# Attention and gated MLP on one core: the start of the x tiles moved by 32 bytes

## The chip, the cores and the metric

One core of a Trainium2 chip runs the whole program. The metric is device time in microseconds (us); a run's time is that of this one core.

## What is computed

```
B, H, S, D = 8, 8, 576, 64          # batch, heads, tokens, head width
scores = q @ k.T / sqrt(D)          # masked: heads 0-3 see 32 tokens back, heads 4-7 every 32nd token back
attn   = softmax(scores);  y = attn @ v
x = y.transpose(0, 2, 1, 3).reshape(B * S, H * D)       # 4608 x 512
h = x @ w_in                                            # 512 -> 2048
sp = max(h, 0) + log1p(exp(-abs(h)));  g = h * erf(sp)
out = g @ w_out                                         # 2048 -> 512, float32
```

## The kernel before

**Staging.** Attention runs a batch entry and a pair of heads at a time (`heads`, L324): scores into PSUM (L400), maximum, difference, exponential, sum and division on the vector, scalar and GpSimd engines, a transpose on TensorE (L507), and the product with v (L526). The result, 128 channels by 576 tokens, is split into two float32r parts that together carry float32 precision: ScalarE casts the upper part into `xhi` (L545), VectorE writes what is left into `xlo` (L550). There are four tiles of each, one per pair of heads, each with room for two batch entries of 576 tokens (`RING`, 1152 words in a partition).

**The MLP** works on chunks of 512 tokens: one chunk for each of the eight batch entries, and a ninth of the 64 tokens that each entry leaves over, which go out to memory (`stash`, L842) and come back (`reload`, L848). A chunk is done in 16 tiles of 128 of the 2048 hidden features (`ftile`, L665). One such f-tile has two groups of 12 matmuls, all 128 x 128 by 128 x 512, on float32r operands:

- `mm1` (L679): the stationary operand is a 128 x 128 block of a `pair` tile of `w_in` (upper or lower part), the moving operand 512 columns of `xhi` or `xlo`, in the order: upper weights with the four `xhi`, lower weights with the four `xhi`, upper weights with the four `xlo`. All 12 add up in one PSUM bank.
- `mm2` (L755): for each of four blocks of 128 tokens, three matmuls. The stationary operand is a 128 x 128 block of `ghi`, `ghi` again, and `glo`; the moving operand is the upper, the lower and again the upper half of a `pair` tile of `w_out`.

Between them ScalarE and VectorE turn h into g in ten passes over 128 x 512 (L687, L693, L684, L717, L720, L723). Over the run `mm1` and `mm2` have 1728 matmuls each, 144 groups of 12.

**Order.** A planner (`Plan`, L158) lays all operations of all engines out in time from tables of keys (`KP`, `KW`, `FT`), costs and buffer counts, and the program is issued in that order. The planner does not know addresses.

**Addresses.** Tiles of a pool lie one after another in each partition, and a tile's size is rounded up to 32 bytes. Pool `cpool` comes first: `xhi` and `xlo` (4608 bytes each), `ident` (512), `con` (1024; masks and a bf16 identity), `con_e` (one word, 32 bytes taken; the zero that the first exponential is taken of, to load ScalarE's table, L803 and L806). In the built program the x tiles start at byte 16512 of a partition, a multiple of 64, and since 4608 is one too, so do all eight, `ident`, `con` and `con_e`. The 32 bytes of `con_e` then put every tile of the later pools, the `pair`, `ghi`, `glo`, `qk`, `sm` tiles and all others, 32 bytes past a multiple of 64. The second batch entry of an x tile starts 2304 bytes on, again a multiple of 64; a block of 128 columns of a stationary operand is 512 bytes wide.

Of the kernel before, what the change touches and what calls it, by code (L numbers as in the profile page):

```python
# [8 lines left out]
F32 = mybir.dt.float32  # L9
# [9 lines left out]
P = 128  # L19
# [247 lines left out]
def attention_moe(  # L267
# [15 lines left out]
    cpool = ctx.enter_context(tc.tile_pool(name="cpool", bufs=1))  # L283
# [4 lines left out]
    ps_h = ctx.enter_context(tc.tile_pool(name="ps_h", bufs=2, space=PSUM))  # L288
    ps_o = ctx.enter_context(tc.tile_pool(name="ps_o", bufs=1, space=PSUM))

    xhi = [cpool.tile([P, RING], F32R, name=f"xhi{c}") for c in range(NCC)]
    xlo = [cpool.tile([P, RING], F32R, name=f"xlo{c}") for c in range(NCC)]
    ident = cpool.tile([P, P], F32, name="ident")
    con = cpool.tile([P, NCON], BF16, name="con")
    con_e = cpool.tile([P, 1], F32, name="con_e")
    mask_l = con[:, :320]
    mask_s = con[:, 320:384].rearrange("p (u q) -> p u q", u=1)
    ident_b = con[:, 384:]
# [688 lines left out]
```

## Time and profile before

| what | value |
|---|---|
| median of 3 runs (lowest to highest) | 940.04 us (939.42 to 943.2) |
| the profiled execution, its own time | 937.79 us |
| its span, first to last instruction | 936.0 us |
| TensorE matmuls busy | 909.9 us (97%) |
| TensorE weight loads busy | 728.6 us (78%) |
| VectorE busy | 680.5 us (73%) |
| ScalarE busy | 687.7 us (73%) |
| GpSimd busy | 69.7 us (7%) |
| DMA, mean rate | 77 GB/s |
| mean granted TensorE clock, share of full speed | 0.995 |

The engines are PE (TensorE's matmuls), PEld (its weight loads, which run beside the matmuls), ACT (ScalarE), DVE (VectorE), POOL (GpSimd) and SP (SyncE, which issues most DMAs). Matmuls are pipelined: the duration of one in the profile covers its way through the array and overlaps with that of the next, so the time that a matmul costs is the distance from its start to the start of the next. In a timeline row that merges several matmuls, the start is that of the first and the duration reaches to the end of the last.

### The profile page before, as it was taken

To read this page: it belongs to the slowest core of one execution; us is meant where nothing else is said; L and a number is where in the kernel's file an instruction comes from. 1 tells how busy PE (TensorE), PEld (TensorE's weight loads), DVE (VectorE), ACT (ScalarE), POOL (GpSimd) and SP (SyncE) were. 2 spreads that over 40 slices of the span, in tenths; PEclk is the share of its full clock that TensorE was granted. 3 is DMA by queue.
4 is the path that set the end of the run, shared out by engine and by line. 5 is a ranking of instruction groups with operands and counts; after the bars stand their busy time and mean duration, and the time that the engine had idled before them with its cause. 6 is when DMAs were issued, how large, how long until landed. Compare 5 with 4: busy or idle time off the path is not lost.

```text
span 936.0 us, 18645 instructions
## 1 busy us (share of the span) xinstructions
PE 909.9 (97%) x7589; PEld 728.6 (78%) x7593; DVE 680.5 (73%) x1111; ACT 687.7 (73%) x1330; POOL 69.7 (7%) x66
## 2 busy tenths in 40 slices
PE   5789999999999999999999999999999999999997
PEld 3567888788878788887878888878888888888885
DVE  7999998988578757766588666685687656665653
ACT  4798988887686767776777668767777687768773
POOL 1310012002021000000010010010001100000000
PEclk9899999999999999999999999999999999999999
DMA  9995123314142202011222021021221310001002
GB/s 346 314 352 210 45 66 52 67 56 99 32 86 72 69 29 103 28 47 48 77 85 68 27 89 46 28 91 34 71 85 41 93 46 1 1 1 45 1 1 45
DMA packets 33557, 72.43 MB, mean 77 GB/s; under 512 B 11968, under 2 KB 12608, under 8 KB 33472
## 3 DMA queue, kind: packets, MB, share of 16 engines
q1 hardware_dynamic: 30016, 64.96, 20.4%
q0 software_dynamic: 3456, 6.29, 3.9%
q8 instruction: 59, 0.97, 0.4%
q14 instruction: 26, 0.21, 0.1%
HBM read 55.51 MB, written 15.73 MB: 76 GB/s over the span
## 4 chain that ended last, share of the span: by engine, by line
PE 83%; issue 5%; DVE 5%; DMA 4%; ACT 2%; SPq 0%; POOL 0%; ACTq 0%; POOLq 0%; DVEq 0%
PE o L755 38%; PE h L679 38%; PE x L526 3%; PE s L400 2%; DMA qk<-qk_str 2%; PE t L507 1%; DVE a L684 1%; ACT a L687 1%; DMA words<-w_in 1%; DMA out<-ob 1%; DVE glo L723 1%; DMA v<-v_str 0%; DVE hs L717 0%; DVE mx L436 0%; PE s L526 0%
## 5 line engine op out<-in xcount | busy, mean ns | idle before, releaser
L755 PE MATMUL o<-pair,ghi 128*128 128x512 f32 x1152 | 364.1, 397 | 0.4 <-ACT ob L771 0.4
L687 ACT ACTIVATE a<-a 128x512 f32<-128x512 f32 x432 | 262.8, 631 | 52.5 <-DVE a L684 51.2
L679 PE MATMUL h<-xhi,pair 128*128 128x512 f32 x1152 | 294.2, 397 | 0.2 <-DVE a L684 0.2
L679 PEld LDWEIGHTS h<-xhi,pair 128*128 128x128 f32 x1152 | 214.7, 188 | 52.2 <-DVE a L684 1.3
L755 PEld LDWEIGHTS o<-pair,ghi 128*128 128x128 f32 x1152 | 211.6, 188 | 46.9 <-ACT ob L771 0.9
L755 PE MATMUL o<-pair,glo 128*128 128x512 f32 x576 | 224.9, 390 | 0.4 <-DVE glo L723 0.2
L679 PE MATMUL h<-xlo,pair 128*128 128x512 f32 x576 | 157.6, 395 | 0.0
L723 DVE TENSOR_TENSOR glo<-hs,ghi 128x512 fp32r<-128x512 f32 x144 | 102.6, 713 | 71.6 <-ACT ghi L720 71.3
L717 DVE TENSOR_TENSOR hs<-a,hs 128x512 f32<-128x512 f32 x144 | 105.7, 734 | 63.5 <-ACT a L687 63.5
L687 ACT ACTIVATE a<-h 128x512 f32<-128x512 f32 x144 | 86.2, 598 | 75.4 <-PE h L679 62.8
L684 DVE SCALAR_TENSOR_TENSOR a<-a,hs 128x512 f32<-128x512 f32 x144 | 99.4, 690 | 47.0 <-ACT hs L693 33.1
L679 PEld LDWEIGHTS h<-xlo,pair 128*128 128x128 f32 x576 | 108.2, 188 | 26.2
L755 PEld LDWEIGHTS o<-pair,glo 128*128 128x128 f32 x576 | 108.2, 188 | 25.2 <-DVE glo L723 1.2
L684 DVE SCALAR_TENSOR_TENSOR a<-h,a 128x512 f32<-128x512 f32 x144 | 98.8, 686 | 31.9 <-ACT a L687 16.9
L693 ACT COPY hs<-h 128x512 f32<-128x512 f32 x144 | 84.3, 585 | 46.4 <-DVE glo L723 43.9
L720 ACT CAST ghi<-hs 128x512 fp32r<-128x512 f32 x144 | 88.4, 614 | 22.2 <-PE o L755 20.8
L684 DVE SCALAR_TENSOR_TENSOR a<-b,a 128x512 f32<-128x512 f32 x144 | 100.5, 698 | 2.1
L687 ACT ACTIVATE b<-a 128x512 f32<-128x512 f32 x144 | 89.9, 624 | 0.4
L498 POOL TENSOR_TENSOR sm<-sm,r 128x768 f32<-128x768 f32 (+3 forms) x37 | 51.0, 1379 | 513.7 <-DVE r L491 478.2
L771 ACT COPY ob<-o 128x512 f32<-128x512 f32 x52 | 30.1, 589 | 9.7 <-DMA out<-ob 4.3
L526 PEld LDWEIGHTS x<-sm,v 64*64 64x64 f32 x1392 | 24.4, 134 | 9.2 <-ACT sm L513 7.0
L436 DVE TENSOR_REDUCE mx<-s 128x12 f32<-128x768 f32 (+3 forms) x37 | 28.9, 782 | 0.3
(50 smaller groups left out, 506.1 us busy)
## 6 DMA issues: line engine op xcount, KB each, us to landing
v<-v_loc SPq DMA_DIRECT2D x13, 640.0 KB, 4.0
words<-w_in SPq DMA_DIRECT2D x16, 512.0 KB, 6.5
words<-w_out SPq DMA_DIRECT2D x16, 512.0 KB, 8.2
out<-ob SPq DMA_DIRECT2D x32, 256.0 KB, 2.0
qk<-qk_loc SPq DMA_DIRECT2D x13, 592.0 KB, 4.1
qk<-qk_str SPq DMA_DIRECT2D x12, 608.0 KB, 3.8
v<-v_str SPq DMA_DIRECT2D x16, 384.0 KB, 3.5
out<-ob POOLq DMA_DIRECT2D x16, 256.0 KB, 5.0
```

Source lines behind the costliest of these rows:

```text
L436: yield nc.vector.tensor_reduce(out=mx[:, parts[i], :units], in_=wide(of(s, i)), axis=mybir.AxisListType.X, op=ALU.max)
L498: yield (nc.gpsimd if pool_norm else nc.vector).tensor_tensor(out=d, in0=d, in1=spread(rc, i), op=ALU.mult)
L526: yield nc.tensor.matmul(bank(px, m)[h * D : (h + 1) * D, a * n : (a + 1) * n], values(rows, (2 * a + h) * D), pt[rows, h, c : c + n], sta ...
L679: yield nc.tensor.matmul(ph[:, :CH], win[4 * s + cc][:, w, fs], x[cc][:, c0 : c0 + CH], start=(i == 0), stop=(i == len(terms) - 1))
L684: yield nc.vector.scalar_tensor_tensor(out=out, in0=in0, scalar=scalar, in1=in1, op0=op0, op1=op1)
L687: yield nc.scalar.activation(dst, src, func, bias=bias[i], scale=scale)
L693: yield nc.scalar.copy(hs.tile, ph.tile)
L717: yield nc.vector.tensor_tensor(out=hs.tile, in0=a.tile, in1=hs.tile, op=ALU.mult)
L720: yield nc.scalar.copy(ghi.tile, hs.tile)
L723: yield nc.vector.tensor_tensor(out=glo.tile, in0=hs.tile, in1=ghi.tile.bitcast(F32), op=ALU.subtract)
L755: yield nc.tensor.matmul(po.tile, g[:, ts], wout[f][:, w], start=(f == first_f and i == 0), stop=(f == last_f and i == 2),)
L771: yield nc.scalar.copy(ob.tile, po.tile)
```

## The change

A tile `shift` of 8 words (32 bytes) is allocated ahead of the x tiles, and `con_e`, which stood behind `con`, becomes its first word.

```diff
+    shift = cpool.tile([P, 8], F32, name="shift")
     xhi = [cpool.tile([P, RING], F32R, name=f"xhi{c}") for c in range(NCC)]
     xlo = [cpool.tile([P, RING], F32R, name=f"xlo{c}") for c in range(NCC)]
     ident = cpool.tile([P, P], F32, name="ident")
     con = cpool.tile([P, NCON], BF16, name="con")
-    con_e = cpool.tile([P, 1], F32, name="con_e")
+    con_e = shift[:, :1]
```

In the program built from it, `shift` starts at byte 16512 and the eight x tiles, `ident` and `con` each start 32 bytes later than before, 32 bytes past a multiple of 64. The later pools start at the same byte as before (54944), and none of their tiles moves. On every engine the same instructions stand in the same order with the same waits; the memset and the first exponential name `shift` where they named `con_e`, and that is all that differs.

## Rows read from the trace of the kernel before

**Rows 1.** The page's list of engines: busy us, share of the span, instructions.
```profile
PE 909.9 (97%) x7589; PEld 728.6 (78%) x7593; DVE 680.5 (73%) x1111; ACT 687.7 (73%) x1330; POOL 69.7 (7%) x66
```

**Rows 2.** Busy time of each engine by stretch; PEclk is the granted clock.
```profile
core 0: us, PE busy (x) PEld busy (x) DVE busy (x) ACT busy (x) POOL busy (x), PEclk, DMA share, GB/s
...
50.00:100.00 50.00, 47.11 (x457) 37.17 (x457) 49.18 (x89) 44.26 (x99) 3.43 (x3) 1.00 0.68 248
100.00:200.00 100.00, 99.56 (x650) 80.32 (x649) 93.67 (x161) 84.89 (x155) 9.64 (x10) 1.00 0.24 52
...
800.00:900.00 100.00, 100.00 (x434) 81.30 (x433) 59.80 (x90) 73.52 (x131) 0.00 (x0) 1.00 0.03 11
```

**Rows 3.** Waits of PE from 100 us on: total us, times, longest us.
```profile
PE x L526 <- ACT sm L513: 0.4, 1, 0.4
PE o L755 <- ACT ob L771: 0.4, 1, 0.4
PE o L755 <- DVE glo L723: 0.2, 1, 0.2
```

**Rows 4.** Groups by form: busy us, mean ns of one | idle us before, releaser.
```profile
L755 PE MATMUL o<-pair,ghi 128*128 128x512 f32 x1152 | 364.1, 397 | 0.4 <-ACT ob L771 0.4
L679 PE MATMUL h<-xhi,pair 128*128 128x512 f32 x1152 | 294.2, 397 | 0.2 <-DVE a L684 0.2
```

**Rows 5.** Timeline of PE, one f-tile of the ninth chunk: start us, us.
```profile
832.34 2.03 PE L679 MATMUL h<-xhi,pair 128*128 128x512 f32 x8
...
835.14 0.63 PE L755 MATMUL o<-pair,ghi 128*128 128x512 f32 x2
835.61 0.39 PE L755 MATMUL o<-pair,glo 128*128 128x512 f32 x1
835.84 0.62 PE L755 MATMUL o<-pair,ghi 128*128 128x512 f32 x2
836.30 0.39 PE L755 MATMUL o<-pair,glo 128*128 128x512 f32 x1
...
837.89 0.40 PE L679 MATMUL h<-xhi,pair 128*128 128x512 f32 x1
```

**Rows 6.** Timeline of PE at the end, a long stretch of `mm2` alone, first and last.
```profile
918.94 0.61 PE L755 MATMUL o<-pair,ghi 128*128 128x512 f32 x2
...
927.10 0.61 PE L755 MATMUL o<-pair,ghi 128*128 128x512 f32 x2
```

**Rows 7.** Timeline of PE, four `mm1` groups in a row, first and last.
```profile
445.80 2.03 PE L679 MATMUL h<-xhi,pair 128*128 128x512 f32 x8
...
454.20 2.03 PE L679 MATMUL h<-xhi,pair 128*128 128x512 f32 x8
```

**Rows 8.** Timeline of PE in an odd chunk, whose x starts 2304 bytes on.
```profile
583.72 2.03 PE L679 MATMUL h<-xhi,pair 128*128 128x512 f32 x8
...
586.52 0.63 PE L755 MATMUL o<-pair,ghi 128*128 128x512 f32 x2
```

**Rows 9.** The matmuls of line 679 by stretch: length, PE busy us (count).
```profile
50.00:100.00 50.00, 25.77 (x106) 1.00 0.68 248
100.00:936.00 836.00, 394.27 (x1596) 1.00 0.18 52
```

**Rows 10.** Groups by form: others that touch the moved tiles.
```profile
L507 PE MATMUL t<-ident,sm 128*128 128x128 f32 x144 | 19.6, 272 | 0.0
L550 DVE TENSOR_TENSOR xlo<-x,xhi 128x324 fp32r<-128x324 f32 x12 | 5.9, 495 | 5.2 <-ACT xhi L545 3.1 <-PE o L755 2.1
```

**Rows 11.** Waits over the whole span: total us, times, longest us.
```profile
ACT a L687 <- PE h L679: 62.8, 77, 4.4
ACT ghi L720 <- PE o L755: 20.8, 26, 2.1
PE warm L885 <- DMA con<-consts: 5.0, 1, 5.0
```

## The prediction

> **What bounds the kernel now.** The list of engines comes first: TensorE's matmuls are busy 97% of the span and its weight loads beside them 78%, no other engine over 73% [rows 1]. [...] The waits of PE agree: from 100 us on there are three, 1.0 us together [rows 3]. Before 100 us PE does wait, for loads and for VectorE. So for nine tenths of the run the time is the sum of what PE's instructions take, and only a change in the pace of its matmuls can move it by much.
>
> Busy time does not tell that pace. A merged row shows `mm1` and `mm2` matmuls of the same form at the same 397 ns [rows 4], but that covers the way through the array, and neighbours overlap. The pace is read from starts in the timeline. One f-tile of the last chunk: 12 `mm1` matmuls run from 832.34 to 835.14, 2.80 us or 233 ns each; the 12 of `mm2` to 837.89, 2.75 us [rows 5]. Within that `mm2` group the first five take 1.16 us (835.14 to 836.30, 232 ns each) and the last seven 1.59 us (227 ns each). At the end, where `mm2` runs alone, the slow start is gone: from 918.94 to 927.10 there are 36 matmuls in 8.16 us, 227 ns each [rows 6]. Where four `mm1` groups follow each other, three take 8.40 us (445.80 to 454.20), again 233 ns each [rows 7]. So `mm1` never reaches the pace that `mm2` settles at; it loses 6 to 7 ns in each matmul, and it leaves `mm2` in a state that takes five matmuls to shed.
>
> What differs? Both move 512 columns of float32r past 128 x 128 weights, both read new weights for each matmul, and nothing waits. In `mm2` the moving tile and the stationary tile both start 32 bytes past a multiple of 64. In `mm1` the weights do, but x starts at a multiple of 64. I take this as the cause: the two streams that TensorE reads at once, the moving columns and the next weights, disturb each other by their relative place within 64 bytes. It is an inference from two paces and two layouts, not something a row shows. One row helps: an odd chunk, whose x starts 2304 bytes on (256 past a multiple of 512), has the same 2.80 us (583.72 to 586.52) [rows 8]; so a step of 256 bytes does nothing, which fits a rule on 64 bytes or less than 256.
>
> **The change part by part.** It adds no instruction, removes none, and moves none past another; every wait stays.
>
> *The moving operand of `mm1`.* x now stands 32 bytes past a multiple of 64, as the weights do. I take the pace of the long `mm2` stretch for it, 227 ns: 12 matmuls in 2.72 us in place of 2.80, 0.08 us less a group. From 100 us on there are 1596 matmuls, 133 groups [rows 9], all on the path: 133 x 0.08 = 10.6 us. The bounds are nothing and, if every `mm1` and `mm2` matmul ran at 227 ns from the start, 5.44 us per f-tile in place of 5.55: 133 x 0.11 = 14.6 us.
>
> *The slow start of `mm2`.* If `mm1` no longer leaves the disturbed state, a `mm2` group after it loses 0.03 us (2.75 against 2.72). But pieces of attention between the groups disturb the pace too. From 100 us on there are 24 pairs of heads with three pieces on PE each, 72, so I count the gain for 133 - 72 = 61 groups: 1.8 us. Against it, a `mm1` group behind such a piece would then have a slow start of its own; for a third of the 72 that is 24 x 0.03 = 0.7 us. Net 1.1 us.
>
> *The first 100 us.* Here PE waits for others, so I count nothing; were all of it on the path, the 106 matmuls at 50 to 100 us [rows 9], 9 groups, would give 0.7 us.
>
> *Others that touch moved tiles.* The transposes move `ident` (192 of them; the 144 of the later batch entries are 19.6 us busy); VectorE reads `xhi` (64 times, 0.4 to 0.5 us), ScalarE writes it [rows 10]. The trace has no second layout of these. By the 3% that separates 2.80 from 2.72 the transposes give or take 0.8 us; I take nothing, since `mm1` is the nearest row but its 512 columns leave far more time for the two streams to meet. VectorE's and ScalarE's parts, 29 us at most each, would shift by 1 us off the path, covered by PE. The load of `con`, for which the first matmul waits 5.0 us [rows 11], keeps its size and queue: nothing, or 0.15 us by the same 3%. The memset and the first exponential on `shift` act on one word as before.
>
> *What is late next.* With an f-tile of 5.44 us, ScalarE's 74 us per 100 us at the end become 75, and VectorE's 94 at 100 to 200 us become 95 [rows 2]. Both wait for PE more than PE for them: ScalarE for h 77 times, 62.8 us, and for `ghi` to come free, 20.8 us [rows 11]. These waits shrink first, so I give back only 0.2 us for the stretch where VectorE is nearly full.
>
> Sum: 10.6 + 1.1 - 0.2 = 11.5 us. The profiled execution's own 937.8 us becomes 926.3. Its span is 936.0 and it lies 2.25 us below the median of the runs, 940.04; the forecast is made for the median: **928.5 us**.
>
> **Rivals.** *No difference by address.* The pace of `mm1` might belong to the loop: 12 different stationary blocks from eight tiles and 12 sums into one bank, where `mm2` uses `ghi` twice in a row and changes bank after three. Then it stays at 2.80 and the time at 940.0. For it: the rows show two loops, never one loop at two addresses. Against it: in `mm2` the pace does not follow the position in its groups of three once it has settled (the last seven are even), and the first five are slow over two banks and all three kinds of operand. [...]
>
> *Half.* What matters is a larger unit, 512 bytes, in which x and weights must agree. In even chunks the new start agrees with the weight blocks (16544 and the `pair` tiles' starts are both 160 past a multiple of 512), in odd ones it is 256 off. Five chunks of nine gain: 5/9 x 11.5 = 6.4 us, 933.6. For it: `mm2`, the only fast pattern, agrees in 512 too. Against it: rows 8, where 256 bytes changed nothing.
>
> *Slower.* The place of x at a multiple of 64 might be the better one, because a row of 2048 bytes then fills whole 64-byte units and 32 past it takes one more; `mm2` would be fast for another reason. The price is the only distance known, 0.08 us a group, the other way: 144 x 0.08 = 11.5, 951.5 us. It decides if a matmul whose moving tile begins off a unit of 64 costs more than one that does not. Against it: every moving tile of `mm2` begins so and has the faster pace.
>
> **How the numbers follow.** Forecast 0.58, half 0.11, no difference 0.21, slower 0.10. The likeliest case alone reaches from 925 (the upper bounds of 14.6 and 0.7 us give 924.7) to 932 (8 us, if `mm1` settles late). Half lies at 933.6, and no difference at 940 give or take the runs' own spread; to hold 8 in 10 the range goes to 941.5, and leaves out the slow case and the outer part of the spread. 0.5% is 4.7 us, about what a measurement of this kernel can tell from no change. The forecast case is faster by more, and nearly all of the half case: 0.67. Same: the no-difference case and the smallest gains, 0.23. Slower 0.10.
>
> **What would show it.** Right: `mm1` groups of 2.72 to 2.73 us with the 5.55 us of an f-tile near 5.45, `mm2` behind `mm1` at 227 ns from its first matmul, VectorE's and ScalarE's busy time unchanged to 1%. Half: 2.72 in even chunks and 2.80 in odd ones. Wrong: `mm1` at 2.80 (no difference) or above it; or `mm1` faster and the span not, with PE waits from 100 us on well over the 1.0 us of now.

## The result, and the profile after

The changed kernel takes 928.6 us (median of 4 runs, 927.63 to 929.62) against 941.57 us (median of 4 runs of the kernel before, 939.42 to 943.2). The ratio on record is 0.9869, with a 95% interval of 0.9841 to 0.9896 (the two medians alone give 0.9862). Two of the four runs before lie at 943.1 and 943.2 us and two at 939.4 and 940.0, so the median before stands between them. The forecast was 928.5 us. The profiled execution took 927.94 us, its span is 926.2 us, 9.8 us less than before.

The list of engines after (busy us, share, instructions) stands against [rows 1]: PE lost 12.0 us of busy time, VectorE and ScalarE are within 0.2% of before.

```profile
PE 897.9 (97%) x7589; PEld 728.4 (79%) x7593; DVE 679.2 (73%) x1111; ACT 687.8 (74%) x1330; POOL 70.1 (8%) x66
```

One f-tile of the ninth chunk in the timeline of PE (start us, us), against [rows 5], and `mm1` of an odd chunk, against [rows 8]. Line numbers are one higher than before.

```profile
851.29 1.98 PE L680 MATMUL h<-xhi,pair 128*128 128x512 f32 x8
...
854.01 0.62 PE L756 MATMUL o<-pair,ghi 128*128 128x512 f32 x2
854.46 0.39 PE L756 MATMUL o<-pair,glo 128*128 128x512 f32 x1
854.69 0.62 PE L756 MATMUL o<-pair,ghi 128*128 128x512 f32 x2
...
856.73 0.62 PE L680 MATMUL h<-xhi,pair 128*128 128x512 f32 x2
```
```profile
573.94 1.98 PE L680 MATMUL h<-xhi,pair 128*128 128x512 f32 x8
...
576.66 0.62 PE L756 MATMUL o<-pair,ghi 128*128 128x512 f32 x2
```

`mm1` takes 2.72 us (851.29 to 854.01, and 573.94 to 576.66 in the odd chunk) where it took 2.80, and `mm2` 2.72 where it took 2.75. The slow start of `mm2` is gone: its first two matmuls take 0.45 us (854.01 to 854.46), where they took 0.47. An f-tile is 5.44 us, as forecast.

PE's waits from 100 us on (total us, times, longest us) grew from 1.0 us [rows 3] to 2.7, and in the table by stretch 100 to 200 us PE's busy time fell from 99.56 to 98.60, while VectorE stayed at 94% there [rows 2].

```profile
PE x L527 <- ACT sm L514: 1.0, 1, 1.0
PE o L756 <- ACT ob L772: 0.9, 1, 0.9
PE h L680 <- ACT hs L694: 0.5, 1, 0.5
PE o L756 <- DVE glo L724: 0.3, 1, 0.3
```
```profile
100.00:200.00 100.00, 98.60 (x652) 80.79 (x651) 93.93 (x161) 84.91 (x155) 9.64 (x10) 1.00 0.25 52
...
800.00:900.00 100.00, 100.00 (x442) 82.80 (x442) 61.15 (x93) 75.01 (x134) 0.00 (x0) 1.00 0.03 11
```

### The profile page after: what moved, and what is told of

Read it like the earlier page. It is cut to its first block, busy times and chain, and to the rows that moved or that the text cites. A ratio compares the mean times of both kernels' runs of the same rounds, so it can differ in the third digit from the quotient of the medians.

```text
span 926.2 us, 18645 instructions
## 1 busy us (share of the span) xinstructions
PE 897.9 (97%) x7589; PEld 728.4 (79%) x7593; DVE 679.2 (73%) x1111; ACT 687.8 (74%) x1330; POOL 70.1 (8%) x66
## 4 chain that ended last, share of the span: by engine, by line
PE 76%; DVE 10%; ACT 6%; issue 5%; DMA 2%; SPq 0%; POOL 0%; ACTq 0%; POOLq 0%; DVEq 0%
PE o L756 36%; PE h L680 34%; DVE a L685 3%; PE x L527 3%; ACT a L688 3%; PE s L401 2%; PE t L508 1%; DMA qk<-qk_loc 1%; DVE w L642 1%; DVE w L636 1%; DVE glo L724 1%; DVE mx L437 1%; DVE pair L650 1%; DMA out<-ob 1%; ACT b L688 1%
## 5 line engine op out<-in xcount | busy, mean ns | idle before, releaser
L680 PE MATMUL h<-xhi,pair 128*128 128x512 f32 x1152 | 287.8, 392 | 1.1 <-ACT hs L694 0.6
L680 PE MATMUL h<-xlo,pair 128*128 128x512 f32 x576 | 154.1, 389 | 0.0
```

The lines of the kernel that those rows point to most:

```text
L680: yield nc.tensor.matmul(ph[:, :CH], win[4 * s + cc][:, w, fs], x[cc][:, c0 : c0 + CH], start=(i == 0), stop=(i == len(terms) - 1))
```

## The experiments

The result fits the forecast, but two paces at two layouts do not prove the cause. The theory: TensorE's two read streams, moving columns and weights, set the pace by their relative place. Rivals: the moving operand's own start decides; or the loop does, and the shift acted in some other way. Still open was the unit, 64 bytes or another.

**A map of matmuls alone (matmul_map).** One loop, two tiles, both 128 bytes past a multiple of 512 in the built program, and only the starts differ:

```python
for name, a, b in MAP:                       # words: x a words on, w b words on
    last = ps.tile([P, DM], F32, tag="acc", name=name)
    for n in range(48):
        c = b + 128 * (n % 4)
        nc.tensor.matmul(last, w[:, c : c + 128], x[:, a : a + 512], start=(n == 0), stop=(n == 47))
```

> Nothing of the reference is computed: 25 stretches of 48 matmuls in a row, each a 128 x 128 stationary block past 512 float32r columns, every one with its own weight load, no other engine at work. The stretches differ only in where the moving operand (x, begins at a multiple of 512) and the stationary operand (w, likewise) start, in bytes: x 0 to 1024 bytes on with w at 0; both 16, 32 or 48 bytes on; w 16, 32 or 48 bytes on with x at 0. If the place of one stream against the other within 64 bytes sets the pace: 227 ns from one start to the next at 0, 64, 128, 256, 512, 1024 and where both are moved alike, 233.5 ns at 32 and 96 and with w at 32, and 16 and 48 show whether it is a matter of 64 bytes or of less. If the moving operand's own start decides: 227 ns for x at 32 and 96 whatever w does, 233.5 ns at 0 and for w at 32. If mm1's pace belonged to its loop (eight weight tiles, 12 sums into one bank) and only its x tiles' shift happened to matter there, all stretches have one pace. Should a start exist with a pace well under 227 ns (the weight load costs nothing there), it is worth trying in the kernel.

Seven of its 25 stretches in the timeline of PE (start us, us; 48 matmuls each; the first row holds the first matmuls of the program, which were slower: with the same starts again, at 282.60 us, a stretch takes 11.17):

```profile
7.42 12.53 PE L41 MATMUL zero<-x,w 128*128 128x512 f32 x48 [7.42 <-ACT x L34]
...
100.36 11.45 PE L41 MATMUL thirtytwo<-x,w 128*128 128x512 f32 x48
...
146.27 11.29 PE L41 MATMUL sixtyfour<-x,w 128*128 128x512 f32 x48
...
169.13 11.43 PE L41 MATMUL onetwentyeight<-x,w 128*128 128x512 f32 x48
180.62 11.17 PE L41 MATMUL twofiftysix<-x,w 128*128 128x512 f32 x48
...
225.76 11.17 PE L41 MATMUL both_thirtytwo<-x,w 128*128 128x512 f32 x48
...
259.57 11.47 PE L41 MATMUL w_thirtytwo<-x,w 128*128 128x512 f32 x48
```

The settled pace, from the starts of the last 24 matmuls of a stretch (ns from start to start):

| x past w, bytes | pace | | others | pace |
|---|---|---|---|---|
| 0, 256, 512, 1024 | 226.7 | | w 32 on, x 0 | 233.3 |
| 32, 96 | 233.3 | | both 32 on | 226.7 |
| 64 | 228.9 | | both 16 or both 48 on | 230.0 |
| 128 | 232.7 | | w 16 on, x 0 | 226.7 |
| 4 | 236.7 | | w 48 on, x 0 | 233.3 |
| 16 | 231.7 | | x 28 on | 226.6 |

The very paces of the kernel, 227 and 233, come back with no other engine at work, one bank and one pair of tiles. x 32 on or w 32 on costs the same, and both 32 on costs nothing: for starts at multiples of 32 it is the distance between the two streams, and the loop is out. The part on 64 bytes missed: 64 and 128 are not as good as 0, and 256 is. No stretch is faster than 226.6 ns.

**All tiles on multiples of 64 (all_on_64).**

```diff
-    con_e = cpool.tile([P, 1], F32, name="con_e")
+    con_e = cpool.tile([P, 16], F32, name="con_e")[:, :1]
```


> Relative place: x, the weights, ghi and glo all start at multiples of 64, none is 32 past another, so mm1 and mm2 both settle at 227 ns, an f-tile of the last chunk takes 5.45 us and the time is that of the changed kernel, 928.6 us within 2 us. The moving operand's own start (32 past 64 is fast): both groups of 12 take 2.80 us, an f-tile 5.60 us, 144 x 0.05 = 7 us more than before, 948 us.

939.83 us, ratio 0.9994 (0.9985 to 1.0004): no gain. One f-tile in PE's timeline:

```profile
851.60 2.03 PE L679 MATMUL h<-xhi,pair 128*128 128x512 f32 x8
...
854.40 0.62 PE L755 MATMUL o<-pair,ghi 128*128 128x512 f32 x2
...
857.14 2.03 PE L679 MATMUL h<-xhi,pair 128*128 128x512 f32 x8
```

`mm1` 2.80 us, `mm2` 2.74: neither expectation. All tiles share their place in 64 bytes, yet only `mm2` is fast. Within 256 bytes x stands at 128 and the weights at 192, 64 apart, while w_out and g both stand at 192. The moving operand's own start within 64 bytes is out too, since x and w_out both start at multiples of 64 here and have two paces.

**x as after the change, the rest moved on (x_off_rest_on).**

```diff
     con_e = shift[:, :1]
+    behind = cpool.tile([P, 8], F32, name="behind")
```


> x as in the changed kernel 32 past 64, all later tiles at multiples of 64. Relative place: mm1 disturbed again (2.80 us), mm2 as in the kernel before (2.75 us), an f-tile of 5.55 us, 941 us as before the change although x starts where the change puts it. The moving operand's own start: mm1 2.72 us, mm2 2.80 us with w_out at a multiple of 64, an f-tile of 5.52 us, 937 us; the order of the two paces within an f-tile tells it apart.

940.74 us, ratio 1.001 (0.9997 to 1.0023).

```profile
852.31 2.03 PE L681 MATMUL h<-xhi,pair 128*128 128x512 f32 x8
...
855.12 0.63 PE L757 MATMUL o<-pair,ghi 128*128 128x512 f32 x2
...
857.86 2.03 PE L681 MATMUL h<-xhi,pair 128*128 128x512 f32 x8
```

`mm1` 2.81 us, `mm2` 2.74: x lies where the change puts it, and the gain is gone, because the weights moved on by the same 32 bytes. This met the theory in time and in the order of the two paces. It takes out the moving operand's own start for any unit, as x has the same bytes here and after the change, and it takes out the tile `shift` itself, which this kernel also has.

**Only the weights on multiples of 64 (weights_on_64).**

```diff
     con_e = cpool.tile([P, 1], F32, name="con_e")
+    ahead = wpool.tile([P, 8], F32, name="ahead")
```


> From the kernel before: x stays at a multiple of 64, and the tiles of w_in and w_out come there too; ghi and glo stay 32 past one. Relative place: the two groups change parts, mm1 settles at 227 ns (2.75 us with the slow start that mm2 now leaves it, at most) and mm2, whose moving w_out is 32 bytes off its stationary g, takes 2.80 us; an f-tile of 5.55 us and 941 us, the same time by the opposite cause. The moving operand's own start: mm1 2.80 and mm2 2.80 us, 948 us.

945.42 us, ratio 1.0055 (1.004 to 1.0071), slower than before.

```profile
854.18 2.03 PE L680 MATMUL h<-xhi,pair 128*128 128x512 f32 x8
...
856.98 0.63 PE L756 MATMUL o<-pair,ghi 128*128 128x512 f32 x2
...
859.78 2.03 PE L680 MATMUL h<-xhi,pair 128*128 128x512 f32 x8
```

Both groups take 2.80 us. `mm2` is slow as the theory said (w_out now 32 bytes past g). `mm1` is not fast, because x and w_in are still 64 apart within 256: the unit of 64 missed here again. Taken alone, this run would have spoken for the moving operand's own start, which gave the same paces and a time 3 us off.

**All tiles on multiples of 64, and in agreement within 256 (all_on_64_agree_256).**

```diff
-    con_e = cpool.tile([P, 1], F32, name="con_e")
+    con_e = cpool.tile([P, 64], F32, name="con_e")[:, :1]
```


> From the kernel before: x stays at its bytes (0 past 64, 128 past 256), and all later tiles move 224 bytes up, so that they too are 0 past 64 and 128 past 256. No tile is 32 past a multiple of 64. If the two streams must agree within 256 bytes (in the map of matmuls 227 ns at a distance of 0, 256, 512, 1024 and 233 at 32, 64 off before, 128): mm1 and mm2 both at 227 ns, an f-tile of 5.45 us, 928.6 us within 2. If agreement within 64 bytes was enough and something else held back the kernel with all tiles on 64, or if a start 32 past 64 is needed: as there, mm1 2.80 us and 940 us.

930.85 us, ratio 0.9906 (0.9885 to 0.9927).

```profile
851.10 1.98 PE L679 MATMUL h<-xhi,pair 128*128 128x512 f32 x8
...
853.82 0.62 PE L755 MATMUL o<-pair,ghi 128*128 128x512 f32 x2
...
856.54 0.84 PE L679 MATMUL h<-xhi,pair 128*128 128x512 f32 x3
```

`mm1` 2.72 us, `mm2` 2.72, though x has not moved and nothing is 32 past a multiple of 64. The intervals of this ratio and of the change's overlap; its median is 0.3 us above the window given, and the last section shows what differed in its profile.

**The change's property kept, the agreement broken (x_64_more, x_128_more).** The comments give the sizes of the second kernel.

```diff
-    shift = cpool.tile([P, 8], F32, name="shift")
+    shift = cpool.tile([P, 24], F32, name="shift")      # x_128_more: 40
...
     con_e = shift[:, :1]
+    behind = cpool.tile([P, 48], F32, name="behind")    # x_128_more: 32
```


> From the changed kernel: x 64 bytes further on, later tiles 256 further. All tiles keep 32 past 64, but x is 64 past the weights within 256. Agreement within 256 bytes: the map has 228.9 ns at +64, so mm1 12 x 228.9 = 2.75 us and mm2 again with a slow start, between 932 and 936 us. Agreement within 64 bytes: no difference to the changed kernel, 928.6 us.

> As the one before, with x 128 bytes further on, so 128 off the weights within 256. Agreement within 256 bytes: the map has 232.7 ns, mm1 12 x 232.7 = 2.79 us, f-tiles of 5.54 us, 939 to 941 us: the whole gain is lost although every tile starts 32 past a multiple of 64, as the change wants it. Agreement within 64 bytes: 928.6 us.

937.52 us, ratio 0.9975 (0.9964 to 0.9985), with x 64 off; 938.34 us, ratio 0.9991 (0.9981 to 1.0), with x 128 off. The f-tile of the second:

```profile
855.32 2.02 PE L681 MATMUL h<-xhi,pair 128*128 128x512 f32 x8
...
858.11 0.63 PE L757 MATMUL o<-pair,ghi 128*128 128x512 f32 x2
...
860.85 1.32 PE L681 MATMUL h<-xhi,pair 128*128 128x512 f32 x5
```

`mm1` 2.79 us, `mm2` 2.74. Every tile still starts 32 past a multiple of 64, and nearly all of the gain is lost. At 128 the time is 0.7 us below the least that was expected. At 64 it came out 1.5 us above the most: there `mm1` sits at 229 ns only after its first four matmuls (237, 235, 232, 232 in the median), and it leaves `mm2` at 230.5 in the mean.

**A finer map (matmul_map_fine).** The same loop, 36 matmuls to a stretch, x 0 to 480 bytes past w.

> Nothing of the reference is computed: 29 stretches of 36 matmuls of the same kind as in the first map, x 0 to 480 bytes past the weights. If 256 bytes is the unit: 288, 320, 384, 448 and 480 have the paces of 32, 64, 128, 192 and 224, and 256 and both streams moved alike by 64 or 416 have 227 ns. If the unit is 512: 288 to 480 differ from them. Moved alike by 8 bytes: 230 ns or more, as 16 and 48 had, if a start between multiples of 32 costs something by itself. I expect no pace under 226.7 ns, since no stretch of the first map had one.

```profile
27.18 8.66 PE L64 MATMUL thirtytwo<-x,w 128*128 128x512 f32 x36
...
44.62 8.53 PE L64 MATMUL sixtyfour<-x,w 128*128 128x512 f32 x36
...
149.20 8.90 PE L64 MATMUL twofourfour<-x,w 128*128 128x512 f32 x36
...
175.40 8.45 PE L64 MATMUL twofivesix<-x,w 128*128 128x512 f32 x36
183.91 8.67 PE L64 MATMUL twoeighteight<-x,w 128*128 128x512 f32 x36
192.64 8.52 PE L64 MATMUL threetwenty<-x,w 128*128 128x512 f32 x36
```

Settled paces: 288 has 233.3 as 32 has, 320 has 228.9 as 64, 448 and 480 have 233.3 as 192 and 224, 384 has 232.1 against 233.3 at 128 (232.7 in the first map). The unit is 256 bytes. Between multiples of it the paces lie from 226.7 (252) to 240.0 (244), without a simple rule. Both streams 64 or 416 bytes on: 226.7; both 8 on: 233.3, so a start between multiples of 32 can cost something by itself. There the distance no longer decides alone. With w 16 bytes on and x at 0, x is 240 past w within 256, and the pace is 226.7; with x 240 on and w at 0 it is 236.7. The rule of 256 is shown for starts at multiples of 32.

```profile
248.36 11.14 PE L41 MATMUL w_sixteen<-x,w 128*128 128x512 f32 x48
```
```profile
140.37 8.78 PE L64 MATMUL twoforty<-x,w 128*128 128x512 f32 x36
```

The first row is of the first map (48 matmuls), the second of the finer one (36). Each map is one execution; the paces at 0, 32, 64 and 240 came out alike in the finer map and in weight_width.

**x moved, `ident` and `con` not (x_alone).**

```diff
+    ident = cpool.tile([P, P], F32, name="ident")
+    con = cpool.tile([P, NCON], BF16, name="con")
     shift = cpool.tile([P, 8], F32, name="shift")
...
-    ident = cpool.tile([P, P], F32, name="ident")
-    con = cpool.tile([P, NCON], BF16, name="con")
```


> The change for x alone: ident and con lie ahead of shift, at multiples of 64 as before the change, and only the x tiles stand 32 past one (160 past 256, as the weights). If the gain is all in the moving operand of mm1: mm1 at 227 ns and 928.6 us within 2 us, as the changed kernel. If ident (transposes) or con (masks) carried a part of it: that part is missing, a time above 930.6 us with mm1 at 227 ns all the same.

930.11 us, ratio 0.9891 (0.9869 to 0.9914).

```profile
850.97 1.98 PE L680 MATMUL h<-xhi,pair 128*128 128x512 f32 x8
...
853.69 0.62 PE L756 MATMUL o<-pair,ghi 128*128 128x512 f32 x2
...
856.41 0.84 PE L680 MATMUL h<-xhi,pair 128*128 128x512 f32 x3
```

`mm1` and `mm2` take 2.72 us each, as after the change. The 144 transposes, whose `ident` is back at a multiple of 64, are busy 19.6 us as they are before and after the change. So x carries the gain; a part of about 1 us for the others cannot be told from noise.

**Narrower weights, and bf16 (weight_width).** The same loop, with `w[:, c : c + cols]` for 128, 64 and 32 columns, and then bf16 copies of both tiles.

> Nothing of the reference is computed: stretches of 36 matmuls as in the maps, with stationary blocks of 128, 64 and 32 columns, x 0, 32, 64, 128, 240 and 244 bytes past the weights; then bf16 operands with 128 columns. [...] If it is the moving stream's own start against some grid: the width changes nothing, 233 and 240 ns at 32 and 244 for all three. With bf16, half the bytes in both streams, I expect a smaller loss or none, 3 ns at most, and a lower pace at 0.

Weight loads by group (busy us, mean ns), and matmuls of bf16 in the timeline (start us, us):

```profile
L65 PEld LDWEIGHTS wide_twofourfour<-x,w 128*128 128x128 f32 x36 | 6.7, 189 | 2.2 <-PE wide_twoforty L65 0.5
...
L65 PEld LDWEIGHTS half_twofourfour<-x,w 128*64 128x64 f32 x36 | 4.9, 138 | 4.0 <-PE half_twoforty L65 0.6
```
```profile
197.37 7.93 PE L65 MATMUL bf_onetwoeight<-xb,wb 128*128 128x512 bf16 x36
205.36 7.93 PE L65 MATMUL bf_twoforty<-xb,wb 128*128 128x512 bf16 x35
```

| x past w, bytes | 128 columns | 64 columns | 32 columns |
|---|---|---|---|
| 0 | 226.7 | 230.0 | 231.7 |
| 32 | 233.3 | 230.8 | 226.7 |
| 64 | 228.9 | 228.3 | 231.1 |
| 128 | 233.3 | 231.1 | 230.5 |
| 240 | 236.7 | 233.3 | 235.5 |
| 244 | 240.0 | 240.0 | 237.8 |

The loads get shorter (189, 138 and 109 ns). If they took a toll on the moving stream in proportion to the weights read, the loss against distance 0 would fall to a half and a quarter and the pace at 0 would fall too; this is the author's estimate, from the widths alone. The loss does fall with them, at 244 from 13.3 to 10.0 and 6.1 ns, at 32 from 6.6 to 0.8 and -5.0, but in part because the pace at 0 rises, from 226.7 to 230.0 and 231.7 ns. The mean of the six paces hardly moves: 233.2, 232.3 and 232.2 ns. So neither such a toll nor the moving stream's own start held as a whole: the width of the block changes the paces, but not in proportion to it. The distance still matters, but the best one depends on the width (64 bytes for 64 columns, 32 bytes for 32). With bf16 every distance has 215.8 ns: all five stretches last 7.93 us.

**All kernels side by side.** Distance of moving operand from weights within 256 bytes, mean ns from start to start from 100 us on (steps over 260 ns, where pieces of attention follow, left out), time:

| kernel | mm1: distance, pace | mm2: distance, pace | median us |
|---|---|---|---|
| before | 224, 233.4 | 0, 229.1 | 939.2 to 941.6 |
| after | 0, 227.1 | 0, 227.7 | 928.6 |
| all_on_64_agree_256 | 0, 227.1 | 0, 227.7 | 930.85 |
| x_alone | 0, 227.1 | 0, 227.7 | 930.11 |
| x_64_more | 64, 230.2 | 0, 230.5 | 937.52 |
| x_128_more | 128, 232.6 | 0, 228.7 | 938.34 |
| all_on_64 | 192, 233.3 | 0, 229.0 | 939.83 |
| x_off_rest_on | 224, 233.4 | 0, 229.1 | 940.74 |
| weights_on_64 | 192, 233.2 | 32, 233.3 | 945.42 |

## Why the prediction was right

*What bounds the kernel.* Held. After the change PE is at 98.6% or more of every 100 us from 100 to 900 us (99.56% or more before), at a granted clock of 1.00 in each of them both times, and the time followed the pace of its matmuls. The end is different: from 900 us on PE was busy 29.30 of the 36 us before, as its last matmul ends some 7 us before the end.

*The moving operand of `mm1`, 10.6 us.* Measured: the steps of `mm1` from 100 us on exceed 227 ns by 9.8 us in total before and by 0.2 us after, so 9.7 us. The pace chosen, that of the long `mm2` stretch, was the right row. The mean steps, 233.4 and 227.1 ns, make 0.075 us a group where the sum took 0.08, which is 0.6 us of the difference; the rest are 48 matmuls ahead of pieces of attention, which the measured figure leaves out.

*The slow start of `mm2`, net 1.1 us.* Undersized: the steps of `mm2` exceed 227 ns by 3.3 us before and 1.0 us after, 2.2 us. The count of 61 was the error. In the trace 93 stretches of `mm2` stand straight behind `mm1`, and they gained 2.1 us, 0.022 us each where the sum took 0.03; the 59 behind a piece of attention gained 0.2. `mm1` stands straight behind such a piece 13 times, not 24, and loses 0.5 us there, which the 9.7 us above contain.

*What is late next, 0.2 us.* Undersized, in the profiled execution: PE's waits from 100 us on grew by 1.7 us, and 100 to 200 us gave back 0.96 us of PE's busy time where VectorE is nearly full. It also began the MLP 0.36 us later than the execution before. So of 11.9 us in pace (9.7 + 2.2) the profiled execution shows 9.85 us (937.79 to 927.94), where the sum said 11.5; the medians show 13.0. The two lie on either side of the forecast, which is as close as run to run variation lets one say. Hitting 928.5 to 0.1 us is partly luck: the first term was too large by 0.9 us and the second too small by 1.1, and the waits grew by more than was given back.

*The cause.* Right in kind, wrong in the unit. "Their relative place within 64 bytes" failed: it is within 256 (all_on_64, x_64_more and x_128_more are counterexamples to 64, the maps show 256). Rows 8 were read too narrowly: a step of 256 bytes that does nothing fits every unit that divides 256, and 256 itself. The change works because 160 past 256 is also where the `pair` tiles begin, not because other tiles are 32 past a multiple of 64. x happened to lie exactly 32 bytes short of agreement within 256, so the same 32 bytes that the rule on 64 asked for were also the right ones; that is luck. *Half*, with a unit of 512, fell: odd chunks have 2.72 us too. *No difference by address* fell with the map, where one loop has both paces: 226.7 ns with both tiles at the same place, 233.3 with either of them 32 bytes on. *Slower*, by a unit more that an offset row touches, fell with both streams 32 on at 226.7.

*Others that touch moved tiles, nothing.* Held as far as it can be told (x_alone).

*Still open.* How the distance acts inside TensorE: whether the weight loads take reads from the running matmul or something else is at work, no run shows. That it is a matter of both streams is shown (x alone or w alone moved by 32 bytes: 233.3 ns, both moved: 226.7); a price in proportion to the weights read is not what weight_width shows. Why a start between multiples of 32 sometimes costs (both 8 on: 233.3 ns) and sometimes does not (w 16 on: 226.7) is open too.

## What to carry to other kernels

Where PE is the bound and matmuls on float32r read new 128-column weights each time, look at the distance between starts in the timeline, not at the duration: two loops of the same form, both of 397 ns in the mean [rows 4], settled here at 227 and 233 ns from start to start, by operand placement alone. Compare the starts of the moving and the stationary tile modulo 256 bytes. With blocks of 128 columns and starts at multiples of 32, equal starts gave the best pace here, 226.7 ns, at the price of some padding; a tile of 32 bytes allocated ahead of one of them was enough to change it for the whole kernel, from 941.57 to 928.6 us. Both tiles 8, 16 or 48 bytes on cost 3 to 7 ns more, and with 64 or 32 columns equal starts were not the best (230.0 and 231.7 ns, where the best had 228.3 and 226.7). With bf16 the five distances tried made no difference (215.8 ns).

## What the runs showed of the hardware that was not expected

*A slow start that remembers.* After a disturbance the steps run through a series before they settle: 231, 236, 228, 233, 231, then 227, in the map with nothing else running (both 32 on), and the same within 1 ns in the median of `mm2` before. It is not always this one: with x 512 bytes on, the map has 240, 235, 234, 235, 225, 230, 236, 229, 232 before it settles at the same 227. With x 28 bytes on, or with w 16 bytes on, the series is nearly absent: these stretches last 11.15 and 11.14 us, the one with both 32 on, at the same settled pace, 11.17. A kernel with such a distance was not tried: what is left of slow starts after the change is 1.2 us (0.2 and 1.0 above), less than a run can tell.

*A longer wait of TensorE, then a lower clock.* In the profile of all_on_64_agree_256 PE comes to the same piece of attention 1.38 us before ScalarE has its data, where it waited 0.44 us in the kernel before and 1.02 us after the change. Timeline of PE, then the table by stretch (columns as in [rows 2]):

```profile
280.20 1.37 PE L526 MATMUL x<-sm,v 64*64 64x32 f32 x72 [1.38 <-ACT sm L513]
```
```profile
275.00:280.00 5.00, 3.83 (x20) 2.86 (x18) 3.79 (x7) 4.70 (x9) 0.00 (x0) 1.00 0.00 0
280.00:285.00 5.00, 4.80 (x82) 3.98 (x83) 3.00 (x6) 3.77 (x9) 0.00 (x0) 0.72 0.45 145
```

After that wait the granted clock is 0.72 in the mean of 280 to 285 us, and three matmuls of `mm2` there (282.40 to 283.68 us) are 427 ns apart. Counted by matmul, this execution lost 2.1 us against the kernel before between the 864th and the 1008th large matmul, and 2.9 us in the first 144 of them, with a granted clock of 0.74 from 60 to 80 us, where the profile after shows 1.00. Together this is most of the 5.25 us by which it lies above the profiled execution after the change (933.19 against 927.94). The profile of x_alone has the earlier fall too, 0.74 from 60 to 80 us, and a wait of 1.35 us at the same piece. The profiles before and after, with 0.44 and 1.02 us of wait there, show 1.00 in both places, 60 to 80 and 275 to 285 us.

The earlier fall is not a matter of the faster pace. x_off_rest_on, whose `mm1` is as slow as before, has it in its profile as well; the first row is of all_on_64_agree_256, the second of x_off_rest_on.

```profile
60.00:80.00 20.00, 17.25 (x188) 13.66 (x182) 17.53 (x33) 14.37 (x29) 1.52 (x1) 0.74 0.91 318
```
```profile
60.00:80.00 20.00, 17.89 (x232) 14.15 (x227) 18.96 (x35) 16.01 (x33) 1.52 (x1) 0.83 0.91 301
```

That the clock explains how far apart the other runs of all_on_64_agree_256 and x_alone lie (929.3 to 933.2 us) is not shown: their mean granted clock goes from 0.985 in the longest to 0.993, but two runs of 932.4 and 929.4 us both have 0.988.
